# Heads 20 to 23 by rows through SyncE, moved memsets and another order of the opening steps of an attention-and-MLP kernel

## The chip, the cores and the metric

The kernel runs on one core of a Trainium2 chip. The metric is the device time of one execution in microseconds (us). The engines are TensorE (PE; PEld is its weight load), VectorE (DVE), ScalarE (ACT), GpSimd (POOL) and SyncE (SP). Each executes its own instructions in order. PE, DVE, ACT and POOL compute. SP issues DMAs and waits for semaphores, and POOL and ACT issue some DMAs as well.

## The reference

```python
def _attn_ref(q, k, v, s):                       # q, k, v: (8, 8, 576, 64); s: (8, 8, 576)
    scores = (1 / np.sqrt(D)) * np.matmul(q, k.transpose(0, 1, 3, 2))
    causal = np.triu(np.ones((S, S), dtype=bool), k=1)
    cum = np.cumsum(np.maximum(s, 0.0), axis=-1)
    bias = -(cum[:, :, :, None] - cum[:, :, None, :])
    scores = np.where(causal, -1e9, scores + np.minimum(bias, 0.0))
    attn = np.exp(scores - np.max(scores, axis=-1, keepdims=True))
    attn = attn / (np.sum(attn, axis=-1, keepdims=True) + 1e-09)
    return np.matmul(attn, v)

def _moe_ref(x, g_ln, w_ch1, w_ch2):             # x: (8, 576, 512), the heads side by side
    xn = (x - mean(x)) / np.sqrt(var(x) + 1e-06) * g_ln
    return x + np.maximum(xn @ w_ch1, 0.0) @ w_ch2     # w_ch1: 512 x 2048, w_ch2: 2048 x 512
```

So there are 8 batches of 8 heads, 64 heads in all, numbered through: head n belongs to batch n // 8. Causal attention with a bias from a cumulative sum is followed, per batch, by a layer norm, a two-layer MLP and a residual.

## The kernel before

**Attention.** Scores are computed transposed: keys on the partitions, queries along the free axis. A head has four full blocks of 128 keys and a last one of 64. The bias is not added: k and q each get four more rows (KA = 68 rows instead of 64) that hold the pieces of the cumulative sum in bf16 (high, middle, low part) and constants, so that the product of the 68 rows is score plus bias. `scores(b, h)` makes three PSUM banks `sa`, `sb`, `sc` and ACT takes the exponential into `er`; `scores_d` does the 64 x 64 corner for two heads. For heads up to 9 the causal mask is added by PE; from head 10 on POOL's `affine_select` (L345, L375) sets the masked part to zero after the exponential. `pv` multiplies with v, into which a column of ones gives the sum of the row, and `pv_norm` divides on DVE.

**Where k and q come from.** A group `gam` is four heads; three buffers `kq` hold k and q of a group, with the head dimension on the partitions. There are three ways into them:

- Batch 0 (groups 0 and 1) comes by tiles of 128 positions, eight heads wide, into `rowb`. PE transposes them (step T), DVE or ACT copies them out (step e).
- Groups 2 to `NPE` - 1 come by pairs of heads. POOL issues a casting DMA for k and one for q (`ld_cast_pair`), PE transposes each in six pieces (`tr_kind`, step Q), two copies on DVE or ACT take the result to `kq` (`evac_half`, step E), and four small DMAs on SP (`aug`) bring the bias rows.
- Groups from `NPE` on come by rows. SP issues ten loads of f32 rows into `rowtmp` (`ld_rows`, L169, k and q of five position tiles), POOL casts them and adds the bias columns (`cast_rows`, L177 and L180), and SP issues three DMA transposes into `kq` (`tr_rows`, L187). The keys and queries then stand in another layout, so `q_cols` splits a matmul that crosses position 512 in two.

`NPE` is 6 before the change, so groups 2 to 5 (heads 8 to 23) come by pairs.

**Layer norm and MLP.** `ln_xn` makes the normalized rows xn of a batch. One DMA transpose on SP (`ln_tr_dma`, L515) makes xT of a batch (from batch 1 on; batch 0 uses PE, step X). `mlp1` makes one of 16 blocks of the hidden layer (four matmuls of 512 columns, L538), `mlp2` a quarter of the second layer's sum for a tile of 128 positions (four matmuls, L557), and after the fourth quarter DVE makes the output tile `yo` and SP stores it. Such units stand in `queue`, and `run_units` takes them from there to fill PE between the steps of attention.

**The order of the work** is written out by hand. Up to head 17 it is the string PLAN: a word names a step, its arguments and perhaps the engine (`:D` DVE, `:A` ACT). The steps that the text speaks of: `W` matmuls on zeros that keep PE busy, `T.t.g` transposes of position tile t for group g, `S`, `x`, `V`, `N` scores, exponential, product with v and division for batch 0, `M.c.t.j` the first pieces of the MLP of batch 0, `Q`/`E` as above, `s.n`, `d.n`, `v.n`, `n.n` scores, corner, product with v and division of head n, `p.n` the function `pre(n)` (loads, `aug`, `tr_rows`, `ld_rows` that are due at head n), `c.n` the function `post(n)` (`cast_rows` that are due), `u` and `U` one unit of the queue, `D` the DMA transpose of batch 1's xT. There are 23 words `u` or `U`; "unit 20" is the 20th, which ends the second layer's sum of the first position tile and so leads to the first output. A loop over heads 18 to 63 follows, in which `pre`, `scores`, units, `post` and `pv_next` follow each other; the first units of batch 1 run at head 20.

POOL's instructions before PLAN (L636 to L682) are a list of DMA issues (k, q, v, weights) with memsets between them. A memset of rows 64 to 127 of `kq[2]` fills what the bias rows of heads 8 to 11 leave free, so the step `aug` waits for it.

SP in the built program before the change sends: s and one tile of k, aug of groups 2, 3, 4 and 5, two outputs, six loads of rows for group 6, xT of batch 1, one output, and on with groups 6 and 7.

Of the kernel before, what the change touches and what calls it, by code (L numbers as in the profile page):

```python
# [9 lines left out]
F32 = mybir.dt.float32  # L10
# [5 lines left out]
P = 128  # L16
# [3 lines left out]
def kernel(  # L20
# [11 lines left out]
    nc = tc.nc  # L32
    B, H, S, D = q.shape
# [5 lines left out]
    NF = S // P  # L39
# [6 lines left out]
    EW = 1664  # L46
    G = 4
    NG = BH // G
    NPE = 6
    NM = 10  # L50
    KT = 96
    QT = 6
# [32 lines left out]
    kq = [const.tile([P, 2, G, SP], BF16, name=f"kq{i}") for i in range(3)]  # L85


    def home(gam):
        return 2 if gam == 2 else gam % 2
# [38 lines left out]
    def tile_src(kind, t):  # L128
        pn = P if t < NF else TL
        src = k if kind == "k" else q  # L130
        return src[0, :, t * P : t * P + pn, :].rearrange("h s d -> s h d")

    def tile_dst(kind, t):
        pn = P if t < NF else TL
        u = "kq".index(kind)
        return rowb[0:pn, t, u * H : (u + 1) * H, 0:D]
# [9 lines left out]
    def ld_cast_tile(kind, t):  # L146
        nc.gpsimd.dma_start(out=tile_dst(kind, t), in_=tile_src(kind, t))

    def ld_cast(kind, g):
        ready[kind, g] = pair_tile(kind)  # L150
        nc.gpsimd.dma_start(out=ready[kind, g][0:QP], in_=pair_src(kind, g))

    def ld_cast_pair(g):
        ld_cast("k", g)
        ld_cast("q", g)

    def ld_cast_v(b, t):
        pn = P if t < NF else TL
        nc.gpsimd.dma_start(  # L159
            out=v_bf[b % 2][:pn, t, :, 0:D],  # L160
            in_=v[b, :, t * P : t * P + pn, :].rearrange("h s d -> s h d"),
        )

    def ld_rows(gam, t):
        pn = P if t < NF else TL
        b, h0 = gam // 2, (gam % 2) * G
        tmp = stage.tile([P, 2, G, D], F32, name="rowtmp", tag="st")
        for u, src in enumerate((k, q)):
            nc.sync.dma_start(  # L169
                out=tmp[0:pn, u],  # L170
                in_=src[b, h0 : h0 + G, t * P : t * P + pn, :].rearrange("h s d -> s h d"),
            )
        loaded["rows", gam, t] = tmp
# [10 lines left out]
    def tr_rows(gam, t0, t1):  # L184
        pn = P if t0 < NF else TL
        o, n = t0 * 2 * G * P, (t1 - t0) * 2 * G
        nc.sync.dma_start_transpose(  # L187
            out=kq[home(gam)]
            .rearrange("p u h s -> p (u h s)")[:, o : o + n * pn]
            .rearrange("p (h s) -> p h s", s=pn),  # L190
            in_=row_sets[gam % 2][0:pn, o : o + n * P],
        )
# [4 lines left out]
    def ld_w1(c):  # L197
        sl = slice(c * 512, (c + 1) * 512)
        nc.gpsimd.dma_start(out=w1_bf[:, :, sl], in_=w1_r[:, :, sl])

    def ld_w2(i):
        nc.gpsimd.dma_start(
            out=w2_bf[:, 4 * i : 4 * i + 4, :], in_=w2_r[:, 4 * i : 4 * i + 4, :]
        )
# [3 lines left out]
    def aug(gam, eng, h0=0):  # L208
        r = slice(gam * G + h0, gam * G + G)
        i = home(gam)  # L210
        eng.dma_start(out=kq[i][D : D + 1, 1, h0:G, 0:S], in_=c_hi[r, :])
        for j in range(3):
            eng.dma_start(out=kq[i][D + 1 + j : D + 2 + j, 0, h0:G, 0:S], in_=c3[r, j, :])
# [80 lines left out]
    def k_cols(b, h, kb):  # L294
        i, hh = home(b * 2 + h // G), h % G
        if b * 2 + h // G < NPE:
            return kq[i][0:KA, 0, hh, kb * P : (kb + 1) * P]
# [4 lines left out]
    def q_cols(b, h, q0, q1):  # L302
        i, hh = home(b * 2 + h // G), h % G
        if b * 2 + h // G < NPE:
            return [(q0, q1, kq[i][0:KA, 1, hh, q0:q1])]
# [330 lines left out]
    for t in range(1, NF):  # L636
        ld_cast_tile("k", t)
        ld_cast_tile("q", t)
        ld_cast_v(0, t - 1)
        if t == 1:  # L640
            make_identity(nc, ident)
        if t == 2:
            nc.gpsimd.memset(maskT, 0.0)
            nc.gpsimd.affine_select(
                out=maskT,
                in_=maskT,
                compare_op=ALU.is_ge,
                fill=-1.0e30,
                base=0,
                pattern=[[1, P]],  # L650
                channel_multiplier=-1,
            )
            nc.gpsimd.dma_start(out=gb, in_=moe_g_ln.partition_broadcast(P))
    ld_cast_v(0, NF - 1)
    ld_w1(0)
    ld_cast_pair(4)
    nc.gpsimd.memset(er[:, :, OD:EW], 0.0)
    nc.gpsimd.memset(v_bf[1][:, 0:NF, :, D : D + 1], 1.0)
    nc.gpsimd.memset(v_bf[1][0:TL, NF, :, D : D + 1], 1.0)
    for i in range(2):  # L660
        nc.gpsimd.memset(v_bf[i][TL:P, NF, :, :], 0.0)
    ld_cast_tile("k", NF)
    ld_cast_tile("q", NF)
    ld_cast_v(0, NF)
    ld_w1(1)
    for u, two in ((0, -1.0058441162109375), (1, 1.0019378662109375)):
        nc.gpsimd.memset(kq[2][D:P, u].bitcast(F32)[:, :, 0 : S // 2], two)
    for i in range(2):
        nc.gpsimd.memset(kq[i][0:KA, 0, :, S:SP], 0.0)
    ld_cast_pair(5)  # L670
# [18 lines left out]
    E = {"A": "act", "D": "dve"}  # L689
# [159 lines left out]

    AUGS = {8: 3, 9: 4, 16: 5}
    PAIR_LOADS = {12: (10, 9), 13: (11,)}


    def pre(n):
        if n == 11:
            ld_w2(2)
            ld_w2(3)
        for g in PAIR_LOADS.get(n, ()):  # L860
            ld_cast_pair(g)
        if n in AUGS:
            aug(AUGS[n], nc.sync)
        for gam in range(NPE, NG):
            if n - 4 * gam == -4:
                for t0, t1 in ((0, 2), (2, NF), (NF, NT)):
                    tr_rows(gam, t0, t1)
        for gam in range(NPE, NG):
            for t in ({-7: (0, 1, 2) if gam == NPE else (0, 1)} if gam % 2 == 0 else {-8: (0, 1), -7: (2, 3), -6: (4,)}).get(n - 4 * gam, ()):
                ld_rows(gam, t)  # L870
        for nb in range(2, B):
            t = n - H * nb + (4 if nb == 2 else 6)
            if 0 <= t < NT:
                ld_cast_v(nb, t)

    def post(n):
        for gam in range(NPE, NG):
            for t in {-6: (0, 1), -5: (2, 3, 4)}.get(n - 4 * gam, ()):
                cast_rows(gam, t)

    def pv_next():
# [56 lines left out]
        "U": lambda: run_units(1, True),  # L938
        "u": lambda: run_units(1),
        "p": lambda n: pre(n),  # L940
        "c": lambda n: post(n),
    }

    PLAN = """
        relu.0 scan.0 relur cq hi.0 scan.1 sub.0 hi.1 ck mid.0 lo.0 W.4 sub.1 mid.1 tc.0 bc.0 W.2
        T.0.0 scan.2 lo.1 hi.2 e.0.0:D T.0.1 W.2 e.0.1:D sub.2 tc.1 S.0.0.0 x.0.0.0 S.0.1.0
        bc.1 V.0.0 T.1.1 mid.2 N.0.0 x.0.1.0 T.1.0 V.0.1 e.1.1:D S.1.1.0 lo.2 m e.1.0:A tc.2 bc.2
        x.1.1.0 S.1.0.0 T.2.0 S.1.1.1 bc.4 T.2.1 e.2.0:D x.1.0.0 S.1.0.1 x.1.1.1 S.2.0.0 T.3.0
        V.1.1 N.0.1 e.2.1:D aug x.2.0.0 x.1.0.1 L.0 S.2.1.0 S.2.0.1 x.2.1.0 S.2.1.1 V.1.0
        e.3.0:D x.2.0.1 T.3.1 N.1.0 N.1.1 S.2.1.2 x.2.1.1 S.2.0.2 x.2.1.2 x.2.0.2 L.1 S.3.0.0  # L950
        X.0 V.2.1 S.3.0.2 N.2.1 y.0:A x.3.0.2 x.3.0.0 S.3.0.1 x.3.0.1 M.0.0.0 e.3.1:D V.2.0
        S.3.0.3 M.0.0.2 S.3.1.3 x.3.0.3 M.0.0.3 N.2.0 M.0.0.1 S.3.1.0 L.2 x.3.1.0 X.1 S.3.1.1
        y.1:D V.3.0 x.3.1.3 X.2 r.0.0:D M.0.1.0 M.0.1.1 T.4.0 N.3.0 S.3.1.2 M.0.1.3 y.2:A
        x.3.1.1 M.0.1.2 Q.k.4 e.4.0:D x.3.1.2 E.k.4.1:D S.4.0.1 r.0.1:A Q.q.4 x.4.0.1 T.4.1
        E.q.4.1:A E.k.4.0:D M.0.2.0 E.q.4.0:A S.4.0.0 M.0.2.2 M.0.2.3 e.4.1:D V.3.1 x.4.0.0
        N.3.1 M.0.2.1 S.4.1.1 L.3 x.4.1.1 s.8 Q.q.5 E.q.5.1:A S.4.1.0 Sk X.3 x.4.1.0 r.0.2:D
        E.q.5.0:A B.1.1 xk u Q.k.5 p.8 y.3:D u s.9 E.k.5.1:D d.8 E.k.5.0:D B.0.1 V.4.0 B.1.0 u u
        p.9 V.4.1 Z N.4.0 s.10 v.8 B.3.0 u u B.0.0 n.8 A.1 Q.q.6 N.4.1 v.9 Q.k.6 E.k.6.0:D
        E.q.6.0:A B.2.0 p.10 E.q.6.1:A E.k.6.1:D p.11 s.11 U n.9 A.0 u d.12 B.2.1 d.10 s.12 U u
        Q.k.7 Q.q.7 p.12 v.10 E.q.7.0:A E.q.7.1:A s.13 B.3.1 u E.k.7.0:D n.10 A.2 A.3 v.11 R  # L960
        E.k.7.1:D u s.14 d.14 n.11 p.13 U v.12 p.14 U O n.12 Q.k.8 g.0 Q.q.8 E.k.8.0:D E.q.8.1:A
        s.15 E.q.8.0:A U E.k.8.1:D u U v.13 Q.k.10 n.13 d.16 E.k.10.0:D p.15 s.16 u E.k.10.1:A
        v.14 n.14 p.16 s.17 Q.k.9 g.1 Q.q.10 U E.k.9.0:D E.q.10.0:A u E.q.10.1:A E.k.9.1:A v.15
        n.15 u g.2 Q.q.9 E.q.9.1:A U Q.k.11 u l.0 p.17 E.q.9.0:A Q.q.11 E.k.11.1:A E.k.11.0:D
        l.2 E.q.11.0:A E.q.11.1:A l.1 l.3 D
    """
    for word in PLAN.split():
        step, _, eng = word.partition(":")
# [6 lines left out]
    for n in range(2 * H + 2, BH):  # L975
# [11 lines left out]
        if h % 2 == 0:  # L987
            scores_d(b, h // 2)
        post(n)
        run_units(0 if late else 1)  # L990
        pv_next()
# [59 lines left out]
```

## Time and profile before

| | |
|---|---|
| time of the runs shown | 352.76 us median of 3 (352.19 to 354.0) |
| the profiled execution | 354.82 us, of which the span from the first to the last instruction is 353.1 |
| PE busy | 344.2 us (97%) in 3066 matmuls |
| DVE, ACT, POOL busy | 192.3, 188.3, 164.9 us |
| chain that ended last | PE 90%, DVE 4%, issue 2%, DMA 1% |
| DMA | 50.96 MB in 171783 packets, mean 144 GB/s |
| SP's queue, POOL's queue | 37.20 MB, 56.4% and 12.46 MB, 42.1% of 16 DMA engines' time |

The page gives the busy time of each engine, the span in 40 slices, the chain of instructions that ended last and groups of instructions by source line. The chain's "issue" is time in which an engine waited for nothing that the profile shows. Matmuls are pipelined and their ends are modelled, so a matmul of 512 columns shows as 379 ns while the next one starts 0.22 us after it.

### The profile page before, as it was taken

The page shows a single profiled execution, that of the slowest core. Times are in us where ns is not written, and L with a number is a line of the kernel's source. Part 1 is how long each engine was busy: PE and PEld are TensorE (multiplying, and loading weights), DVE is VectorE, ACT ScalarE, POOL GpSimd, SP SyncE. Part 2 cuts the span into 40 slices and gives each one's busy share as a digit, 9 for nine tenths or more (in the row PEclk, how much of TensorE's full clock was granted, in tenths as well). Part 3 has the DMA queues.
Part 4 walks back from the last instruction along what each step waited for, and adds up shares of the span by engine and source line. Part 5 has one row for each costly group of instructions (what it writes and reads, how often), then busy time and mean ns, then how long its engine had stood idle before and what let it go on. Part 6 is the DMA issues. An engine that isn't in the chain of part 4 may idle for free.

```text
span 353.1 us, 8167 instructions
## 1 busy us (share of the span) xinstructions
PE 344.2 (97%) x3066; PEld 196.5 (56%) x3090; DVE 192.3 (54%) x517; ACT 188.3 (53%) x360; POOL 164.9 (47%) x336
## 2 busy tenths in 40 slices
PE   8998999999999999999999999999999999999995
PEld 3897856555555455555555555555555544444444
DVE  7884788974366536653565549443844492113112
ACT  4797897957634674366616653576346502502500
POOL 8997578267465628465647275365621010000000
PEclk9998999999999999999999999999999999999999
DMA  9999999999999999999999999999740024011013
GB/s 140 170 176 140 199 203 125 144 186 182 183 180 164 215 164 180 215 223 181 182 177 213 162 192 203 195 173 198 144 125 2 3 65 128 2 59 59 2 31 89
DMA packets 171783, 50.96 MB, mean 144 GB/s; under 512 B 159520, under 2 KB 167136, under 8 KB 171744
## 3 DMA queue, kind: packets, MB, share of 16 engines
q1 hardware_dynamic: 117792, 37.20, 56.4%
q0 software_dynamic: 52432, 12.46, 42.1%
q10 hardware_dynamic: 1520, 0.79, 0.9%
q8 instruction: 24, 0.39, 0.5%
q14 instruction: 15, 0.12, 0.1%
HBM read 37.11 MB, written 9.44 MB: 132 GB/s over the span
## 4 chain that ended last, share of the span: by engine, by line
PE 90%; DVE 4%; issue 2%; DMA 1%; SPq 1%; POOL 1%; ACT 0%; POOLq 0%; DVEq 0%
PE py L557 32%; PE ph L538 31%; PE pot L403 7%; PE sc L325 3%; PE sa L325 3%; PE sb L325 3%; PE ph L820 2%; PE idle L612 2%; PE st L718 2%; DMA rowtmp<-in_q_dram 1%; PE trqk L275 1%; PE pot L776 1%; PE trt L696 1%; DVE xb L417 1%; DVE yo L568 1%
## 5 line engine op out<-in xcount | busy, mean ns | idle before, releaser
L557 PE MATMUL py<-w_bf,hT 128*128 128x512 bf16 (+2 forms) x584 | 130.9, 367 | 1.3
L538 PE MATMUL ph<-xT,w_bf 128*128 128x512 bf16 x480 | 112.6, 379 | 0.3 <-DVE hT L546 0.3
L548 ACT ACTIVATE hT<-ph 128x512 bf16<-128x512 f32 x102 | 60.8, 598 | 73.9 <-PE ph L538 73.9
L557 PEld LDWEIGHTS <-hT 128*128 128x128 bf16 x608 | 54.3, 98 | 52.6
L538 PEld LDWEIGHTS <-w_bf 128*128 128x128 bf16 x544 | 49.5, 98 | 51.6 <-issue 1.0
L336 ACT ACTIVATE er<-sa 128x512 bf16<-128x512 f32 x56 | 33.4, 596 | 63.4 <-PE sa L325 47.1
L345 POOL TENSOR_SCALAR_AFFINE_SELECT er<-er 128x256 bf16<-128x256 bf16 x108 | 45.4, 442 | 29.7 <-ACT er L336 28.9
L546 DVE TENSOR_SCALAR hT<-ph 128x512 bf16<-128x512 f32 x34 | 23.5, 691 | 57.9 <-PE ph L538 49.9
L568 DVE SCALAR_TENSOR_TENSOR yo<-py,rstd,xb 128x512 f32<-128x512 f32 x32 | 23.9, 748 | 35.2 <-PE py L557 33.9
L325 PEld LDWEIGHTS <-kq 68*128 68x128 bf16 x400 | 28.6, 97 | 21.7 <-issue 1.6
L403 PEld LDWEIGHTS <-er 128*128 128x128 bf16 x840 | 32.8, 98 | 13.0 <-POOL er L345 1.2
L403 PE MATMUL pot<-v_bf,er 128*128 128x65 bf16 x840 | 35.1, 194 | 0.4 <-POOL er L345 0.4
L159 POOL DMA_DIRECT2D v_bf<-in_v_dram x40 | 34.3, 864 | 2.0 <-PE pot L403 1.4
L336 ACT ACTIVATE er<-sc 128x512 bf16<-128x512 f32 x56 | 34.2, 611 | 0.0
L336 ACT ACTIVATE er<-sb 128x512 bf16<-128x512 f32 x56 | 33.5, 598 | 0.0
L177 POOL CAST kq<-rowtmp 128x512 bf16<-128x512 f32 (+1 forms) x25 | 15.7, 628 | 36.2 <-DMA rowtmp<-in_q_dram 36.1
L177 POOL CAST rowb<-rowtmp 128x512 bf16<-128x512 f32 (+1 forms) x25 | 15.3, 610 | 34.8 <-DMA rowtmp<-in_q_dram 19.5
L415 DVE RECIPROCAL rinv<-pot 128x5 f32<-128x5 f32 x56 | 10.8, 192 | 37.0 <-PE pot L403 37.0
L417 DVE TENSOR_TENSOR xb<-pot,rinv 128x256 f32<-128x256 f32 x56 | 23.8, 425 | 1.9
L493 DVE SCALAR_TENSOR_TENSOR xn<-xb,mv,gb 128x512 bf16<-128x512 f32 x28 | 22.9, 819 | 1.0
L325 PE MATMUL sa<-kq 68*128 68x512 bf16 x56 | 21.3, 381 | 1.5 <-issue 1.5
L447 DVE BATCH_NORM_STATS2 stats<-xb 128x6 f32<-128x128 f32 (+1 forms) x84 | 21.9, 321 | 0.3
(115 smaller groups left out, 354.4 us busy)
## 6 DMA issues: line engine op xcount, KB each, us to landing
out_dram<-yo SPq DMA_DIRECT2D x32, 256.0 KB
rowtmp<-in_k_dram SPq DMA_DIRECT2D x40, 128.0 KB
rowtmp<-in_q_dram SPq DMA_DIRECT2D x40, 128.0 KB
v_bf<-in_v_dram POOLq DMA_DIRECT2D x32, 128.0 KB, 5.7
w_bf<-in_moe_w_ch_dram POOLq DMA_DIRECT2D x8, 512.0 KB, 11.0
kp<-in_k_dram POOLq DMA_DIRECT2D x8, 144.0 KB, 7.9
qp<-in_q_dram POOLq DMA_DIRECT2D x8, 144.0 KB, 8.1
rowtmp<-in_k_dram SPq DMA_DIRECT2D x10, 64.0 KB
```

What stands on the lines that cost most here:

```text
L159: nc.gpsimd.dma_start(out=v_bf[b % 2][:pn, t, :, 0:D], in_=v[b, :, t * P : t * P + pn, :].rearrange("h s d -> s h d"),)
L177: nc.gpsimd.tensor_copy(out=rows[gam % 2][0:pn, t, :, :, 0:D], in_=loaded.pop(("rows", gam, t))[0:pn])
L325: nc.tensor.matmul(a[:, c + a0 - q0 : c + a1 - q0], lhsT=k_cols(b, h, kb), rhs=cols, start=True, stop=not (pe_mask and diag),)
L336: nc.scalar.activation(out=e[:, o : o + 512], in_=a, func=ACT.Exp, scale=scale)
L345: nc.gpsimd.affine_select(out=two, in_=two, compare_op=ALU.is_ge, fill=0.0, base=0, pattern=[[0, 2], [1, P]], channel_multiplier=-1,)
L403: nc.tensor.matmul(pot[:, t, :], lhsT=e[:, o : o + P], rhs=vv[:, kb, h, :], start=(kb == 0), stop=(kb == last),)
L417: nc.vector.tensor_tensor(out=xb[b][:, :, hs], in0=pot[:, 0:NF, 0:D], in1=rinv[:, 0:NF].unsqueeze(2).to_broadcast([P, NF, D]), op=ALU.mult,)
L538: nc.tensor.matmul(ph, lhsT=w1_bf[:, kd, fb * P : (fb + 1) * P], rhs=xT[:, :, kd, :], start=(kd == 0), stop=(kd == KD - 1),)
L546: nc.vector.tensor_scalar_max(out=hT[:, fb, :], in0=ph, scalar1=0.0)
L548: nc.scalar.activation(out=hT[:, fb, :], in_=ph, func=ACT.Relu)
L557: nc.tensor.matmul(py[t], lhsT=hT[:, fb, t * P : (t + 1) * P], rhs=w2_bf[:, fb, c0:c1], start=(fb == 0), stop=(fb == FB - 1),)
L568: nc.vector.scalar_tensor_tensor(out=yo, in0=py[t], scalar=rs, in1=x[:, c0:c1], op0=ALU.mult, op1=ALU.add)
```

## The change

- `NPE` becomes 5, so group 5 (heads 20 to 23) comes by rows: ten loads and three DMA transposes on SP and ten copies on POOL, in place of two pairs (four casting DMAs on POOL, 24 transposes on PE, eight copies on DVE and ACT) and aug of group 5. The loads are due at heads 14 and 15, the casts at 15 and 16, the transposes at 17. `q_cols` splits the matmuls of these heads.
- POOL's list before PLAN: `ld_w1(0)` comes ahead of the v tile 3; the memset of `kq[2]` comes right after pair 4, ahead of the last tiles of k, q and v; the memsets of `er` and `v_bf` come behind them.
- PLAN has another order. Up to step s.8 it holds the same PE steps; two copies of step e go from DVE to ACT (e.0.1, e.4.0) and two of step y from ACT to DVE. Q and E of pairs 10 and 11 are gone, c.15 and c.16 are new.
- In the loop, the two units that run ahead of the scores of every fourth head now run at head 24 too.

SP in the built program after the change sends: s and one tile of k, aug of groups 2, 3 and 4, ten loads of rows for group 5, one output, three transposes for group 5, six loads for group 6, one output, xT of batch 1, one output, and on. Each DMA of SP also waits for the one eight places before it.

```diff
-    NPE = 6
+    NPE = 5
...
+    ld_w1(0)
     ld_cast_v(0, NF - 1)
-    ld_w1(0)
     ld_cast_pair(4)
+    for u, two in ((0, -1.0058441162109375), (1, 1.0019378662109375)):
+        nc.gpsimd.memset(kq[2][D:P, u].bitcast(F32)[:, :, 0 : S // 2], two)
+    ld_cast_tile("k", NF)
+    ld_cast_tile("q", NF)
+    ld_cast_v(0, NF)
+    ld_w1(1)
     nc.gpsimd.memset(er[:, :, OD:EW], 0.0)
     nc.gpsimd.memset(v_bf[1][:, 0:NF, :, D : D + 1], 1.0)
     nc.gpsimd.memset(v_bf[1][0:TL, NF, :, D : D + 1], 1.0)
     for i in range(2):
         nc.gpsimd.memset(v_bf[i][TL:P, NF, :, :], 0.0)
-    ld_cast_tile("k", NF)
-    ld_cast_tile("q", NF)
-    ld_cast_v(0, NF)
-    ld_w1(1)
-    for u, two in ((0, -1.0058441162109375), (1, 1.0019378662109375)):
-        nc.gpsimd.memset(kq[2][D:P, u].bitcast(F32)[:, :, 0 : S // 2], two)
...
-    AUGS = {8: 3, 9: 4, 16: 5}
-    PAIR_LOADS = {12: (10, 9), 13: (11,)}
+    AUGS = {8: 3, 9: 4}
+    LD_FIRST = {-6: (0, 1), -5: (2, 3, 4)}
+    CAST_FIRST = {-5: (0, 1), -4: (2, 3, 4)}
+    PAIR_LOADS = {12: (9,)}
...
-            if n - 4 * gam == -4:
+            if n - 4 * gam == (-3 if gam == NPE else -4):
                 for t0, t1 in ((0, 2), (2, NF), (NF, NT)):
                     tr_rows(gam, t0, t1)
         for gam in range(NPE, NG):
-            for t in ({-7: (0, 1, 2) if gam == NPE else (0, 1)} if gam % 2 == 0 else {-8: (0, 1), -7: (2, 3), -6: (4,)}).get(n - 4 * gam, ()):
+            for t in ({-7: (0, 1, 2) if gam == NPE + 1 else (0, 1)} if gam % 2 == 0 else LD_FIRST if gam == NPE else {-8: (0, 1), -7: (2, 3), -6: (4,)}).get(n - 4 * gam, ()):
                 ld_rows(gam, t)
...
-            for t in {-6: (0, 1), -5: (2, 3, 4)}.get(n - 4 * gam, ()):
+            for t in (CAST_FIRST if gam == NPE else {-6: (0, 1), -5: (2, 3, 4)}).get(n - 4 * gam, ()):
                 cast_rows(gam, t)
...
     PLAN = """
...
-        S.3.0.3 M.0.0.2 S.3.1.3 x.3.0.3 M.0.0.3 N.2.0 M.0.0.1 S.3.1.0 L.2 x.3.1.0 X.1 S.3.1.1
-        y.1:D V.3.0 x.3.1.3 X.2 r.0.0:D M.0.1.0 M.0.1.1 T.4.0 N.3.0 S.3.1.2 M.0.1.3 y.2:A
...
-        Q.k.7 Q.q.7 p.12 v.10 E.q.7.0:A E.q.7.1:A s.13 B.3.1 u E.k.7.0:D n.10 A.2 A.3 v.11 R
-        E.k.7.1:D u s.14 d.14 n.11 p.13 U v.12 p.14 U O n.12 Q.k.8 g.0 Q.q.8 E.k.8.0:D E.q.8.1:A
-        s.15 E.q.8.0:A U E.k.8.1:D u U v.13 Q.k.10 n.13 d.16 E.k.10.0:D p.15 s.16 u E.k.10.1:A
-        v.14 n.14 p.16 s.17 Q.k.9 g.1 Q.q.10 U E.k.9.0:D E.q.10.0:A u E.q.10.1:A E.k.9.1:A v.15
-        n.15 u g.2 Q.q.9 E.q.9.1:A U Q.k.11 u l.0 p.17 E.q.9.0:A Q.q.11 E.k.11.1:A E.k.11.0:D
-        l.2 E.q.11.0:A E.q.11.1:A l.1 l.3 D
...
+        S.3.0.0 M.0.0.3 M.0.0.2 x.3.0.0 N.2.0 M.0.0.1 S.3.1.3 x.3.0.3 X.1 r.0.0:D x.3.1.3
+        S.3.1.1 S.3.1.0 T.4.0 V.3.0 y.1:D M.0.1.0 M.0.1.3 L.2 M.0.1.2 x.3.1.1 x.3.1.0 S.3.1.2
+        N.3.0 X.2 y.2:D M.0.1.1 Q.k.4 e.4.0:A x.3.1.2 S.4.0.1 Q.q.4 r.0.1:A M.0.2.0 x.4.0.1
...
+        B.2.1 n.8 Q.k.6 E.q.6.1:A E.k.6.1:D s.11 E.k.6.0:D U v.9 U d.12 d.10 n.9 s.12 u u Q.k.7
+        p.12 s.13 B.2.0 E.k.7.0:D B.0.1 v.10 Q.q.7 n.10 E.k.7.1:D A.0 p.13 E.q.7.1:A E.q.7.0:A U
+        A.2 u v.11 A.3 R s.14 p.14 c.15 n.11 u u v.12 U d.14 s.15 Q.q.8 u n.12 v.13 E.q.8.1:A
+        g.0 U Q.k.8 U p.15 n.13 E.k.8.1:D c.16 v.14 E.k.8.0:D g.1 E.q.8.0:A O U s.16 n.14 d.16
+        Q.k.9 u E.k.9.1:A p.16 v.15 Q.q.9 n.15 p.17 E.k.9.0:D E.q.9.0:A g.2 l.3 u E.q.9.1:A l.0
+        s.17 U l.1 l.2 U D
     """
```

## The prediction

> **What bounds the kernel now.** I read four views in turn: the page's busy shares, the engines' busy time over stretches of one clock period, TensorE's (PE's) timeline at its gaps, and the timelines of GpSimd (POOL) and SyncE (SP) around the instructions that release those gaps.
>
> ```profile
> PE 344.2 (97%) x3066; PEld 196.5 (56%) x3090; DVE 192.3 (54%) x517; ACT 188.3 (53%) x360; POOL 164.9 (47%) x336
> ...
> PEclk9998999999999999999999999999999999999999
> ...
> 26.70:30.11 3.41, 1.93 (x40) 1.59 (x37) 2.54 (x8) 2.03 (x5) 3.41 (x6) 1.00 1.36 144
> 30.11:33.52 3.41, 3.41 (x50) 3.41 (x47) 0.42 (x1) 3.36 (x7) 2.56 (x4) 0.50 2.61 142
> ```
>
> PE is the bound: it executes in order, and the time is its work plus its gaps. The last two lines (busy us of PE, PEld, DVE, ACT, POOL, then clock, DMA share, GB/s) show the one bad spot: PE works 1.93 of 3.41 us, and the next 3.41 us run at clock 0.50, so 1.7 us of work are lost there.
>
> ```profile
> 27.20 0.40 PE L718 MATMUL st<-kq 68*128 68x64 bf16 x8
> 29.07 0.38 PE L325 MATMUL sa<-kq 68*128 68x512 bf16 x1 [1.48 <-issue]
> ...
> 18.82 2.12 POOL L667 MEMSET kq<- 64x1152 f32 x2
> ...
> 20.96 0.76 SPq L211 DMA_DIRECT2D kq<-c  x1
> 21.78 1.82 SPq L213 DMA_DIRECT2D kq<-c  x3
> ```
>
> The gap stands before step s.8 (head 8). It is the bias rows of heads 8 to 11 (step aug): SP sends them at 20.96, as POOL's memset of the same rows ends at 20.94, and their last packet leaves at 28.3.
>
> Later the loads matter. Pair 7's k and q (issued at 34.20 and 35.95) took 11.3 and 10.3 us to land, so 45.5 and 46.3, and PE transposes them at 47.56: 2.1 us of slack. The last spot:
>
> ```profile
> 64.76 2.00 SPq L586 DMA_DIRECT2D out_dram<-yo  x2
> ...
> 70.06 0.51 SPq L169 DMA_DIRECT2D rowtmp<-in_q_dram  x1
> 71.79 1.88 SPq L515 DMA_TRANSPOSE xT<-xn  x1
> ...
> 75.71 0.62 PE L403 MATMUL pot<-v_bf,er 128*128 128x65 bf16 x15
> 76.23 1.02 PE L538 MATMUL ph<-xT,w_bf 128*128 128x512 bf16 x4
> ```
>
> SP issues two outputs, six loads of head rows, then the transpose of batch 1's xT. The first matmul that reads this xT starts at 76.23, 4.4 us after the issue; in the trace's semaphore events the last part of xT lands at 76.19. So PE meets it with no slack.
>
> **Part by part: the sum.** It is made on the profiled execution: span 353.1, 354.82 with what lies outside.
>
> *PE work.* Four tr_kind steps go: 24 transposes, 12 of which take 0.51 us on the chain, so -1.0 us. Heads 20 to 23 now read k and q in the split form: head 28's eight matmuls take 0.66 us (111.63 to 112.29) where head 20's five take 0.65, so +0.04 for four heads. Eight copies of 0.80 leave ACT and DVE (six and two); both are half idle, so nothing. The four issues of aug 5 (0.6 each) leave SP. POOL gains 4.1 us of casts (five of 0.61 and five of 0.21) and loses four issues of 0.63; its busy share in 50 to 70 leaves room, and the casts stand behind the masks of s.14 and s.15 and ahead of those of s.16, which PE reads only after 65. Nothing, if the rows have landed by then.
>
> *The memsets.* The memset of the bias rows starts where the memset of er did, 14.27, and ends at 16.4; the rows, with the same 7.4 us from there to the last packet, arrive at 24. PE's work from 6.5 to s.8 is the same set of steps, so s.8 could come at 27.4. But the new order puts T.4.0 before V.3.0, M.0.1.x and X.2: 1.15 us of PE work earlier, 22.05 instead of 23.20. It reads row tile 4, whose q part was issued at 16.73 and took 6.3 us: 23.03. With its issue 0.35 later (2.12 us of memset instead of 1.77) that is 23.0 to 23.4. PE waits there 1.0 to 1.4 us, and s.8 follows 5.15 us of work later, at 28.5: 0.6 earlier than before. The first weights ahead of a v tile, the swapped evacuations (two to ACT, two to DVE, 0.4 to 1.0 us each) lie under PE's work, and cost up to 0.5 if they don't.
>
> *The clock.* With that gap halved and moved to an earlier stretch I take the half-speed stretch as gone: -1.7 us by pair 7.
>
> *Pair 7.* Q.k.7 keeps its place: 16.7 us of work after s.8, so 45.2. That is before the data of 45.5, and the data come later too. SP now sends ten loads of rows as soon as aug 4 is out, from about 36, while POOL's queue is full (204 GB/s in 36 to 46). There a packet of POOL's queue takes 90 ns (2227 packets, 124.6% of 16 engines, 10 us), one of SP's 18 ns (2404 packets, 110.5%, 69.5 to 72). In 87 to 93, where both queues are loaded, they moved 2381 and 3063 packets, so about turn by turn. Equal turns make POOL's queue 20% slower: 9.5 us become 11.4, and pair 7 lands at 47.4. Bounds: 45.5 with no delay, 48.3 at 30%. I take 47.5 for Q.k.7, level with 47.56 before: what the opening gained goes into this wait.
>
> The Trainium skill ("DMA: Bandwidth & Descriptors", queues, rings and completion order) says that each DMA engine takes turns between its queue rows by whole packets of several descriptors. By that rule the delay could be several times mine if SP's turns hold more descriptors; the 87 to 93 row speaks for nearly equal ones.
>
> *xT.* From Q.k.7 to the end of unit 20, which feeds the first output, there are 15.0 us of work: 62.5 (before: 63.70). From there SP in the new program does: output, three transposes for heads 20 to 23, six loads, output, xT. Rows: 1.06 us until the output is issued (63.70 to 64.76) and 0.4 for it; three transposes 6.7 (the set of 95.59; others 6.3 to 9.2, and 5.6 from the median and shortest rows); six loads 3.8 (66.81 to 70.57); one output 0.4; xT until the first reader 4.4. That is 16.7 us, between 15.3 and 18.3. PE has 12.7 us of work in the same stretch (12.53 before). So the first reader waits 4.0 us and starts at 62.5 + 16.7 = 79.2 instead of 76.23: +3.0. PE's queue stands behind it whole. The work that follows is the same.
>
> A gap of 4.0 us is longer than the one at 27.6, so the half clock comes back after it. Part of the slow stretch lies in the gap itself: 0 to 1.7 us, I take 1.2.
>
> Sum: +3.0 + 1.2 = +4.2 us of 353.1, from -0.3 (Q.k.7 at 45.6, chain 15.3, no slow clock) to +7.2 (48.3, 18.3, 1.7). The profiled execution stands 2.06 above the median of the timed runs (352.19 to 354.0); I carry the difference over: 352.76 + 4.2 = 357.0.
>
> The Trainium skill ("TensorE: Matmul & The Clock Gate", why this matters for your kernels) asks for no gaps over about 3 us in PE's work, or the clock drops. By that rule the 1.48 us gap would have been free and only the xT wait is charged; the trace gated after 1.93 busy of 3.41, so here the measurement decides, and the shorter waits at T.4.0 and Q.k.7 may be charged too (second rival).
>
> **The rivals.**
> *Faster: the new SP order has room.* If the three transposes take 5.6 us or less, the loads go out behind them without waiting, and pair 7 lands at 45.5, PE never waits for xT: 60.6 + 12.7 = 73.3 for the first reader, -2.9, and 349.9. It decides at a chain under 12.7 us, and no set of three transposes in this trace is short enough with the rest. For it: loads at 36 find SP idle for 20 us, so the casts are early. Chance 0.12.
> *Slower still: the waits add up.* Rows are served in longer turns, so pair 7 lands 2 us later than I say, the transposes take 7.9 as at 78.12 while v tiles share the engines, or the waits at T.4.0 and Q.k.7 gate the clock: +2.5 to +4 on the forecast, 360. Chance 0.17.
> *No change that can be told: the xT wait is small.* Q.k.7 at 45.6 and a chain of 15.3 give a first reader at 75.9, and a slow clock of 0 to 1.7: 352.5 to 354. For it: DVE is freed of copies, so outputs may be ready sooner. Chance 0.21.
> *The forecast,* a late xT between 75.9 and 81 with its clock: 354.5 to 359. Chance 0.50.
>
> **How the numbers follow.** 0.5% (1.8 us) is about what a measurement of this kernel can tell from no change. Slower by more: 0.50 + 0.17 + 0.02 of the small wait = 0.69; within: 0.19; faster: 0.12. The range leaves out most of the faster case and the top of the slower one: 351.0 to 361.0; the likeliest case alone has 354.5 to 359.
>
> **What would show it.** Right: no gap before s.8 over 0.5 us and clock 1.00 in 30 to 33.5; a gap before T.4.0 near 22 and one before Q.k.7 near 45; SP's xT transpose issued 12 us or more after unit 20's end, and a gap of 2 to 6 us before the first L538 matmul of batch 1, with a slice of PEclk under 9 behind it. Wrong: xT issued before 72, no gap there, and PE's busy sum down by 1 us with nothing in its place.

## The result, and the profile after

The kernel after takes 363.06 us (median of 5 runs, 362.47 to 364.7), the kernel before 352.40 us (5 runs, 351.32 to 354.0). The ratio is 1.031, with a 95% interval of 1.027 to 1.035: slower by 3.1%, some 10.7 us. The profiled execution of after took 363.06 us, with a span of 361.3.

From the page: the busy times of the engines, the granted clock in 40 slices, the shares of the chain that ended last.

```profile
PE 345.3 (96%) x3078; PEld 195.0 (54%) x3078; DVE 193.5 (54%) x517; ACT 182.8 (51%) x352; POOL 164.7 (46%) x342
...
PEclk9999999996999999999999999999999999999999
...
PE 76%; DMA 11%; POOL 5%; SPq 3%; DVE 2%; issue 2%; POOLq 0%
```

PE is not busier in any way that matters (345.3 us against 344.2, and its clock is halved for longer). The chain changed: DMA has 11% of it instead of 1%, SP's queue 3% instead of 1%. One slice of the clock is at 6, the one from 81 to 90 us. The opening, which had the slow stretch before, is clean.

PE's timeline at the place where batch 1's MLP begins:

```profile
70.42 0.19 PE L403 MATMUL pot<-v_bf,er 128*128 128x65 bf16 x1 [1.76 <-DMA v_bf<-in_v_dram]
...
75.74 0.62 PE L403 MATMUL pot<-v_bf,er 128*128 128x65 bf16 x15
82.34 6.14 PE L538 MATMUL ph<-xT,w_bf 128*128 128x512 bf16 x16 [5.98 <-DMA xT<-xn]
88.32 0.38 PE L325 MATMUL sa<-kq 68*128 68x512 bf16 x1
```

Up to 75.74 PE runs level with the kernel before (s.20 starts at 75.03, before at 75.00). Then it stands for 5.98 us, until xT has landed; before, its first reader started at 76.23. The clock of the same stretch (us, busy PE, PEld, DVE, ACT, POOL, clock, DMA share, GB/s):

```profile
76.50:80.66 4.16, 0.00 (x0) 0.00 (x0) 1.48 (x5) 0.72 (x3) 3.32 (x9) 1.00 1.31 229
80.66:84.08 3.42, 1.74 (x5) 0.64 (x5) 0.00 (x0) 0.00 (x0) 0.00 (x0) 0.50 1.40 258
84.08:87.49 3.41, 3.41 (x10) 1.21 (x9) 0.69 (x1) 0.60 (x1) 2.90 (x6) 0.50 1.16 190
```

The clock is halved from 80.66 to 87.49, and PE is busy for 5.15 us of it. So the sixteen matmuls behind the wait take 5.98 us until s.21.

SP's timeline shows what xT stood behind:

```profile
44.49 3.24 SPq L169 DMA_DIRECT2D rowtmp<-in_q_dram  x1
...
62.66 0.37 SPq L586 DMA_DIRECT2D out_dram<-yo  x1
63.22 8.72 SPq L187 DMA_TRANSPOSE kq<-rowb  x3
72.00 0.58 SPq L169 DMA_DIRECT2D rowtmp<-in_k_dram  x1
...
75.42 0.44 SPq L586 DMA_DIRECT2D out_dram<-yo  x1
75.97 3.47 SPq L515 DMA_TRANSPOSE xT<-xn  x1
```

The first output is issued at 62.66 and the transposes of heads 20 to 23 take SP 8.72 us. Then come the six loads and an output, and only at 75.97 xT, though its rows xn were ready near 71.1. It is read 6.4 us later. The first line is one of the ten row loads: where a load took SP about 0.5 us before, these took up to 3.24 each, and the last of the ten landed at 64.67.

### The profile page after: what moved, and what is told of

Its sections match the earlier page's. It is cut to its first block, busy times and chain, and to the rows that moved or that the text cites. A ratio compares the mean times of both kernels' runs of the same rounds, so it can differ in the third digit from the quotient of the medians.

```text
span 361.3 us, 8183 instructions
## 1 busy us (share of the span) xinstructions
PE 345.3 (96%) x3078; PEld 195.0 (54%) x3078; DVE 193.5 (54%) x517; ACT 182.8 (51%) x352; POOL 164.7 (46%) x342
## 4 chain that ended last, share of the span: by engine, by line
PE 76%; DMA 11%; POOL 5%; SPq 3%; DVE 2%; issue 2%; POOLq 0%
PE ph L538 31%; PE py L557 29%; PE pot L403 5%; SPq L169 3%; DMA rowtmp<-in_q_dram 3%; DMA xT<-xn 3%; PE sc L325 3%; PE sa L325 3%; PE sb L325 3%; DMA rowb<-in_q_dram 2%; DMA kq<-c 2%; POOL rowb L147 2%; DMA v_bf<-in_v_dram 1%; POOL v_bf L159 1%; POOL kq L658 1%
## 5 line engine op out<-in xcount | busy, mean ns | idle before, releaser
L557 PE MATMUL py<-w_bf,hT 128*128 128x512 bf16 (+2 forms) x608 | 134.0, 368 | 0.0
L538 PE MATMUL ph<-xT,w_bf 128*128 128x512 bf16 x480 | 114.8, 385 | 6.8 <-DMA xT<-xn 6.8
L345 POOL TENSOR_SCALAR_AFFINE_SELECT er<-er 128x256 bf16<-128x256 bf16 x108 | 44.5, 431 | 32.4 <-ACT er L336 31.6
L325 PEld LDWEIGHTS <-kq 68*128 68x128 bf16 x412 | 29.4, 97 | 20.8 <-issue 0.5
L177 POOL CAST rowb<-rowtmp 128x512 bf16<-128x512 f32 (+1 forms) x30 | 18.3, 611 | 35.7 <-DMA rowtmp<-in_q_dram 31.3
L415 DVE RECIPROCAL rinv<-pot 128x5 f32<-128x5 f32 x56 | 10.7, 191 | 33.8 <-PE pot L403 33.8
L493 DVE SCALAR_TENSOR_TENSOR xn<-xb,mv,gb 128x512 bf16<-128x512 f32 x28 | 24.7, 882 | 1.0
L325 PE MATMUL sc<-kq 68*128 68x256 bf16 (+1 forms) x200 | 21.7, 226 | 0.0
```

What stands on the lines that cost most here:

```text
L177: nc.gpsimd.tensor_copy(out=rows[gam % 2][0:pn, t, :, :, 0:D], in_=loaded.pop(("rows", gam, t))[0:pn])
L325: nc.tensor.matmul(a[:, c + a0 - q0 : c + a1 - q0], lhsT=k_cols(b, h, kb), rhs=cols, start=True, stop=not (pe_mask and diag),)
L345: nc.gpsimd.affine_select(out=two, in_=two, compare_op=ALU.is_ge, fill=0.0, base=0, pattern=[[0, 2], [1, P]], channel_multiplier=-1,)
L493: nc.vector.scalar_tensor_tensor(out=xn, in0=tiles[t], scalar=mvs[b][:, t, 0:1] if b > 0 else mean0[:, t : t + 1], in1=gb, op0=ALU.subtrac ...
L538: nc.tensor.matmul(ph, lhsT=w1_bf[:, kd, fb * P : (fb + 1) * P], rhs=xT[:, :, kd, :], start=(kd == 0), stop=(kd == KD - 1),)
L557: nc.tensor.matmul(py[t], lhsT=hT[:, fb, t * P : (t + 1) * P], rhs=w2_bf[:, fb, c0:c1], start=(fb == 0), stop=(fb == FB - 1),)
```

## The experiments

All times below are medians; each ratio is to the kernel before, run beside it on the same chip (its medians were 352.4 to 353.6). "Transposes" is the time from the first to the end of the last of group 5's three on SP; the last two columns are the issue of xT and the start of its first reader on PE, all from the profiled executions.

| kernel | us | ratio (95%) | transposes | xT issued | first reader |
|---|---|---|---|---|---|
| before | 352.4 | | none | 71.79 | 76.23 |
| after | 363.06 | 1.031 (1.027 to 1.035) | 8.7 | 75.97 | 82.34 |
| e1 memsets | 352.37 | 0.999 (0.997 to 1.001) | none | 69.62 | 74.07 |
| e2 rows | 361.97 | 1.024 (1.020 to 1.028) | 8.6 | 76.42 | 80.97 |
| e3 order, pairs | 359.61 | 1.017 (1.012 to 1.023) | none | 71.84 | 81.88 |
| e4 xT ahead of loads | 358.05 | 1.014 (1.010 to 1.017) | 8.6 | 72.12 | 77.02 |
| e5 busy while waiting | 362.21 | 1.027 (1.022 to 1.033) | 8.8 | 75.47 | 83.18 |
| e6 new opening | 354.12 | 1.003 (1.000 to 1.006) | none | 72.01 | 76.44 |
| e7 rows cast by DMA | 364.57 | 1.033 (1.031 to 1.036) | 8.9 | 76.22 | 83.03 |
| e8 loads early | 362.79 | 1.029 (1.025 to 1.033) | 9.0 | 78.14 | 83.86 |
| e9 e4, old opening | 357.52 | 1.016 (1.012 to 1.019) | 9.3 | 72.97 | 77.42 |
| e10 half the rows | 361.74 | 1.027 (1.023 to 1.031) | 7.4 | 74.40 | 80.95 |
| e11 transposes alone | 361.81 | 1.027 (1.022 to 1.031) | 7.4 | 76.39 | 80.95 |
| e12 loads alone | 357.56 | 1.014 (1.010 to 1.019) | none | 73.34 | 77.89 |
| e13 v tile later | 362.08 | 1.024 (1.019 to 1.029) | 7.8 | 77.62 | 82.98 |
| e14 half, v later | 360.30 | 1.019 (1.015 to 1.023) | 7.4 | 75.67 | 80.88 |
| e15 after again | 363.82 | 1.031 (1.027 to 1.034) | 8.6 | 75.87 | 82.89 |

Theory A, behind most of the expectations: the transposes and loads that stand ahead of xT in SP's queue cause the loss. Its rivals were the order of the plan (C) and the fill of the DMA engines (D).

**e1: the memsets alone, in the kernel before.**

```
+    ld_w1(0)
     ld_cast_v(0, NF - 1)
-    ld_w1(0)
     ld_cast_pair(4)
+    for u, two in ((0, -1.0058441162109375), (1, 1.0019378662109375)):
+        nc.gpsimd.memset(kq[2][D:P, u].bitcast(F32)[:, :, 0 : S // 2], two)
...
```

> The kernel before with one part of the change: the list of POOL instructions ahead of the plan (memset of the bias rows early, first weights ahead of a v tile). Theory A (the opening is a plain gain and the loss comes from the rows alone): the gap of 1.48 us before s.8 falls under 0.4 us, the granted clock is 1.00 in 30 to 33.5, T.4.0 waits up to 0.8 us, and the time falls by 1.5 to 3 us, to 349.5 to 351. Rival B (given back later): s.8 comes 1 us or more earlier, but Q.k.7 then waits for pair 7, which still lands near 45.5 to 46.5, and the time is within 1 us of 352.4.

The gap before s.8 went, s.8 came at 28.17 (before 29.07), the clock was 1.00 in 30 to 33.5, and every later step came 2 to 3 us earlier than in the profile of before: the span is 350.1. Yet the median moved by 0.7 us, which can't be told from nothing. Of the 13 runs of before beside it, all had a mean clock of 0.997 or more, where the profiled execution had 0.995. That execution was slower than all 13 of them (351.33 to 354.13). The slow stretch that the change removes there hardly occurs in the timed runs. Theory A has the profile and not the time; rival B has the time and not its reason, for Q.k.7 does not wait.

**e2: the rows alone, in the kernel before.**

```
-    NPE = 6
+    NPE = 5
...
-        ... Q.k.10 ... E.k.10.0:D ... Q.k.11 ...
+        ... c.15 ... c.16 ...
```

> The kernel before with only heads 20 to 23 taken by rows (loads due at heads 14 and 15, casts at 15 and 16, transposes at 17); POOL's list and the order of the plan stay. Theory A (xT of batch 1 stands on SP behind the three transposes and six loads): the first matmul that reads it starts at 81 to 83.5 instead of 76.2, the clock halves after it, and the time is 360 to 364, so all of the loss is here. Rival C (the new order of the plan is what costs): the first reader comes at 77 to 79 and the time is 353 to 356.

Theory A holds in the time: 8.9 us of the 10.7, with the old order and the old POOL list. The place is only partly as expected. The first reader came at 80.97, but 3.75 us were already lost at 71.40, where v.16 waited for a v tile that POOL had issued behind the casts of late rows:

```profile
71.40 0.19 PE L403 MATMUL pot<-v_bf,er 128*128 128x65 bf16 x1 [3.75 <-DMA v_bf<-in_v_dram]
```

**e3: the new order with pairs.** Heads 20 to 23 go back to pairs in the new plan, with the steps Q and E of pairs 10 and 11 put in by hand.

> The kernel after with heads 20 to 23 put back to pairs (24 transposes on PE, eight copies, bias rows by four DMAs on SP); POOL's list and the new order of the plan stay. Theory A: SP has no rows to load before 60 and sends xT at 71 to 73; its first reader starts within 0.5 us of 75 to 77 and the clock stays at 1.00 behind it; 349.5 to 353. Rival C (the order costs): the waits at T.4.0 and at the pairs add up, and the time is 355 or more.

It took 359.61 us (ratio 1.017), which reads as the rival. But in its profile PE waits 1.11 and 1.69 us at those inserted transposes, for work on ACT, and the clock halves behind them. So it measures where I put the steps and not the order of the change. e6 takes its place for the steps up to s.8.

**e6: the new order up to s.8 only,** with the plan of before from there on, on e1.

> The kernel of the first experiment (the kernel before with the changed list of POOL) with the new order of the plan up to step s.8, and the old order from there on; heads 20 to 23 come by pairs. Theory A (the new order of the opening costs only its wait at T.4.0): s.8 comes 0.5 to 1.3 us later than in the first experiment (28.17), and the time is 352.5 to 354. Rival C (the new order of the opening costs much): 355 or more.

354.12 us, ratio 1.003 (1.000 to 1.006) against 0.999 (0.997 to 1.001) for e1, so about 1.4 us, at the edge of what these runs can tell. PE's timeline shows what it is:

```profile
24.20 0.36 PE L696 MATMUL trt<-ident,rowb 96*68 96x96 bf16 x4 [1.87 <-DMA rowb<-in_k_dram]
25.17 0.36 PE L696 MATMUL trt<-ident,rowb 96*68 96x96 bf16 x4 [0.61 <-DMA rowb<-in_q_dram]
```

T.4.0 stands too early for the tile that it reads. So the opening is not the bulk of the loss; what it costs fits this wait. No run tests the order behind s.8 and the two units at head 24 by themselves. e2, which has the old order, leaves 1.8 us of the 10.7 for them, the opening and POOL's list together.

**e4: xT ahead of group 6's loads,** in the kernel after: the six loads due at p.17 are issued behind D.

```
-        s.17 U l.1 l.2 U D
+        s.17 U l.1 l.2 U D G          (G issues the loads; pre(17) no longer does)
```

> The kernel after with one thing changed: the six loads of rows for heads 24 to 27 go out on SP behind the transpose of batch 1's xT instead of ahead of it. Theory A (order on SP): xT is issued at 72 to 72.5 instead of 75.97, its first reader starts at 78 to 79 instead of 82.34, the slow clock shrinks from 2.6 to some 1.2 to 2 us, and the time is 357 to 359.5. Rival D (the DMA engines are full, so xT lands when the backlog is through): the first reader comes within 1.5 us of 82.3 and the time is 361.5 or more.

```profile
62.84 8.54 SPq L187 DMA_TRANSPOSE kq<-rowb  x3
...
72.12 3.07 SPq L515 DMA_TRANSPOSE xT<-xn  x1
```

xT goes 3.9 us earlier, its reader 5.3 us earlier than in after, the clock stays at 1.00, and 5 us of the 10.7 come back by moving six loads behind one DMA. So theory A holds for this half. What remains in its profile are waits at v.16 (1.5 us, for a v tile), at xT (1.2), at head 20's product with v (1.4, for a mask on POOL behind casts of group 6, whose loads are now later) and at the next part of xT (0.9).

**e11: the three transposes alone,** added to e1, where nothing needs them.

```
     def pre(n):
+        if n == 17:
+            tr_extra()        # tr_rows of group 5's sizes, from rowb into kq[2]
```

> The kernel of the first experiment (old order, changed list of POOL, heads 20 to 23 by pairs, 0.999 of the time before) with three DMA transposes more on SP, of the same size as group 5's, put where the change has them: between the outputs and group 6's six loads. Their result is not used; no load, cast or step of PE is added. Theory A (these transposes on SP ahead of xT are the cost): they take 6.3 to 8.8 us, xT is issued at 75.5 to 78.5 instead of 69.6, its first reader starts at 80 to 83 instead of 74.1, and the time is 358 to 363. Theory D (the row loads and casts are the cost): the transposes take less than 6 us with nothing else in flight, and the time is 352 to 356.

SP's timeline, then PE's:

```profile
64.67 7.38 SPq L860 DMA_TRANSPOSE kq<-rowb  x3
...
76.39 2.43 SPq L515 DMA_TRANSPOSE xT<-xn  x1
```

```profile
80.95 5.48 PE L538 MATMUL ph<-xT,w_bf 128*128 128x512 bf16 x16 [6.89 <-DMA xT<-xn]
86.27 0.38 PE L325 MATMUL sa<-kq 68*128 68x512 bf16 x1
```

Three instructions on SP that no computing engine executes cost 2.7%. xT is issued 6.8 us later than in e1 and read 6.9 us later (74.07 to 80.95), and the clock halves. That is the main mechanism by itself, without loads, casts or another order.

**e12: the ten row loads alone,** added to e1; nobody reads them.

> The kernel of the first experiment with ten loads of rows more on SP, where the change has them (due at heads 14 and 15). Nobody reads them; no cast, transpose or step of PE is added, and the pairs of heads 20 to 23 are still loaded, so this is the loads on top of everything. Theory D (the loads' bytes delay what POOL loads behind them): pairs 9 to 11 land at 60 to 66 instead of 56 to 59.5, PE waits for them, and the time is 355 to 360. Theory A (only SP's order ahead of xT costs): the loads are out of SP by 57, xT is issued within 1 us of 69.6, and the time is 352 to 354.

357.56 us, a ratio of 1.014, so theory D has a part too:

```profile
58.93 0.43 PE L275 MATMUL trqk<-ident,kp 96*128 96x96 bf16 x6 [1.95 <-DMA kp<-in_k_dram]
```

The pairs land late, and SP, held up in the loads, sends the bias rows, outputs and loads behind them late, so xT goes at 73.34. These loads are on top of the pairs, where the change puts them in the pairs' place, so this may overstate what they cost there.

**e10: half the rows,** in the kernel after.

```
-        for u, src in enumerate((k, q)):
+        for u, src in enumerate((k,) if gam == NPE else (k, q)):
```

> The kernel after with only the five loads of k for heads 20 to 23; their q rows are made from the k rows, so half of the loaded bytes and five of SP's issues are left out, and the scores of these heads are other numbers. Everything else stays. Theory D (the loads' bytes fill the DMA engines, so casts, v tile and the transposes come late): the last cast ends by 62, the v tile of head 16 is hardly waited for, the three transposes take 7.5 us or less, the first reader of xT comes at 79 to 81, and the time is 358.5 to 361.5. Theory A (SP's order alone; a set of three transposes takes as long in any case): the casts come earlier, but the transposes still take 8.3 to 9 us from their start near 63, the first reader stays at 81.5 to 83, and the time is 362 to 363.5.

361.74 us, with an interval that overlaps that of after. The transposes took 7.4 us instead of 8.7, v.16 no longer waited, and the first reader came at 80.95 instead of 82.34. Between the theories: the bytes of the loads may be worth up to 1.3 us in the transposes. This rests on one profile each, and e13 below, with all the rows, has 7.8.

**e7: the rows by casting DMAs** on POOL, in the kernel after: `nc.gpsimd.dma_start` from k and q straight into the bf16 rows, without `rowtmp` and without the casts.

> The kernel after with the rows of heads 20 to 23 loaded by ten casting DMAs of POOL straight into the bf16 rows, in place of ten f32 loads on SP and five casts on POOL; the copies of the bias columns, the transposes and all orders stay. It writes half the bytes and no instruction of POOL waits for the loads. Theory G (the f32 row loads fill the DMA engines, so casts, v tile and transposes come late): the rows land by 62, the v tile of head 16 is not waited for, the three transposes end at 69 to 70 instead of 72, xT is issued at 72.5 to 74.5, its first reader starts at 77.5 to 79.5, and the time is 356.5 to 360. Theory A without G (SP's order alone): the transposes still end at 71 or later and the time is 361 to 363.

The forecast of theory G fails: no cast waits for a load any more, and the transposes still take 8.9 us and the first reader comes at 83.03. But its condition was not met either. POOL issues these loads at 53.02 to 61.76, where SP had them at 38.24 to 56.81, and the last lands at 66.2 by the trace's semaphore events, after the 64.67 of the kernel after and not by 62. So this run does not decide on theory G. POOL's ten issues of 0.67 to 0.81 us stand ahead of the v tiles, v.16 waits 2.57 us, and the clock halves there as well.

**e8: group 6's loads early,** ahead of the first output, in the kernel after; one v tile moved ahead of casts.

> The kernel after with group 6's six loads on SP ahead of the first output and of group 5's transposes (they were between these and xT), and the v tile that stood behind the last casts of group 5 on POOL ahead of them. Theory A: xT is issued near 71.5 to 72.5 and its first reader starts at 76.5 to 77.5, as in the experiment with these loads behind xT; the waits for the v tile of head 16 (1.5 us) and for the mask at 89 (1.4 us), which that one had, go, and the time is 354.5 to 357. Rival D (more loads in the full DMA engines make the rows of group 5 later still): the transposes end after 72.5 and the time is 358 or more.

Rival D holds: SP is still in the loads at 67, the first output goes at 67.15 instead of 62.66, and the transposes end at 77.4. The v tile that was issued 8.5 us earlier (58.38) landed at 70.95, no earlier than before its move (70.38). Here, with six more loads in the queues at the same time, issuing it earlier did not deliver it earlier.

**e9: e4 with the old opening.**

> The kernel of the fourth experiment (the kernel after with group 6's six loads behind xT, 1.0135 of the time before) with the old order of the plan up to step s.8. Theory A (the new opening's wait at T.4.0 costs 1.1 to 1.8 us, as the sixth experiment has it, and adds to the rest): 356 to 357. Rival (the gain of the opening is given back at the waits for xT and the v tile, which end when DMAs land): 357.5 to 358.5.

357.52 us, ratio 1.016 (1.012 to 1.019), against 1.014 for e4. The time is the rival's, and its reason is not shown. In this profile the old opening gained nothing that could be spent later: T.4.0 waits 0.72 and 0.63 us here too, and s.8 comes at 29.09, against 28.50 in e4.

**e5: PE kept busy while it waits,** in the kernel after.

```
+        if late: keep_warm(26)
         run_units(2 if late else 0, True)
```

> The kernel after with 26 matmuls on zeros (512 columns, some 0.22 us each, 5.7 us in all) put ahead of the first matmul that reads batch 1's xT, so that PE is busy while it waits. Nothing else is changed. Theory A (the wait itself costs 6.1 us and the slow clock behind it 2.6): the first reader still starts near 82.3, the granted clock is 1.00 throughout, and the time falls by 2 to 3 us, to 360 to 361. Rival E (the clock's part is small, since other engines set the pace while PE is slow): the clock is 1.00, but the time is 362 to 363.5. Rival F (the matmuls on zeros delay what follows): more than 363.5.

```profile
75.78 5.77 PE L612 MATMUL idle<-zeros 128*128 128x512 bf16 x26
83.18 3.69 PE L538 MATMUL ph<-xT,w_bf 128*128 128x512 bf16 x16 [1.63 <-DMA xT<-xn]
86.71 0.38 PE L325 MATMUL sa<-kq 68*128 68x512 bf16 x1
```

With PE busy the clock stays at 1.00, and from the first reader to s.21 it takes 3.53 us instead of 5.98: the half clock costs 2.45 us. In this execution xT came 0.84 us later than in after, so the span gained only 1.4. The medians differ by less than 1 us and their intervals overlap (1.022 to 1.033, 1.027 to 1.035), so the time alone does not settle it; the two profiles do, for this stretch.

**e13, e14, e15: what made xT itself slow.** In after, e5, e7 and e10 xT took 6.4 to 7.7 us from its issue to its reader, and POOL issued a v tile some 2 us behind it. e13 sends that tile 10 us later, e14 does the same with half the rows, e15 is the kernel after again.

```
-            if 0 <= t < NT: ld_cast_v(nb, t)
+            for tt in {(3, 1): (), (3, 2): (1, 2)}.get((nb, t), (t,)): ...
```

> The kernel after with one v tile of batch 3, which POOL issued at 77.70, 1.7 us behind the transpose of xT, issued together with the next v tile at head 20 (near 87). Theory V (that v tile shares the DMA engines with xT and holds it up): xT takes 4.4 to 5 us from its issue to its first reader instead of 6.4, the first reader starts at 80 to 81.2, and the time falls by 1 to 2 us against the kernel after. Rival W (the six loads that stand right ahead of xT on SP hold it up): it stays at 6 us or more, and the time is that of the kernel after within 0.8 us.

> The kernel of the experiment with half the rows (only k is loaded for heads 20 to 23, q is made from it) with the same v tile moved. Theory V with D: both terms that the prediction's chain had too small are gone; transposes 7 to 7.6 us, xT 4.4 to 5 us to its first reader, which starts at 78.5 to 79.8, where the prediction had it (79.2), and the time is 2.5 to 4 us under that of the kernel after. Rival W: first reader at 80.5 or later, and at most 2 us under the kernel after.

> The kernel after, unchanged, beside the two others on the same chip: 362 to 364.5 us, transposes 8.2 to 9 us, xT 6 to 7 us from its issue to its first reader at 81.5 to 83.5, clock 0.985 to 0.991. If xT takes 5 us or less here, the v tile is no cause and the term varies from run to run.

xT to its reader: 7.0 us in e15, 5.4 in e13, 5.2 in e14. So without this v tile it is 1.0 to 1.8 us shorter than in after and e15. But a v tile behind xT is not enough: in before, e1, e2, e6, e11 and e12 POOL issued one 1.9 to 2.7 us behind xT as well, and there xT took 4.4 to 4.6 us. What sets these six apart on SP is that no output goes out right ahead of xT. In after, e5, e7, e10 and e15 an output of 256 KB goes 0.5 to 0.6 us ahead of it and a v tile follows (6.4 to 7.7 us); with such an output and no v tile right behind (e4, e8, e9, e13, e14) it is 4.5 to 5.7. No run moves the output alone, so its part stays open.

The first readers came later than expected: 82.98 in e13 (80 to 81.2) and 80.88 in e14 (78.5 to 79.8). In e13's profile the clock halves from 25.51 to 28.93, behind waits of 1.06 and 0.50 us at T.4.0, and s.8 comes at 31.99. In time e13 is 0.7% under e15, with intervals that overlap, and e14 1.1%, with intervals that don't (ratios 1.024, 1.019 and 1.031).

## Why the prediction was right or wrong

It forecast slower by way of a late xT, and that is what happened, by the mechanism that it named: SP's order output, transposes, loads, output, xT, and a half clock behind the wait. The size was wrong: 357.0 (351 to 361) against 363.06. The steps, in its order:

- *Memsets, s.8 and the first half clock.* The gap before s.8 went (0.22 us left), the clock is 1.00 in 30 to 33.5, T.4.0 waits 0.74 and 0.85 (forecast 1.0 to 1.4). s.8 came at 29.51 instead of 28.5; other executions of the same opening had 28.50 to 29.26 (seven), and 30.39 to 31.99 (e6, e13, e14). Right in kind. But the 1.7 us were credited against an execution that was slower than the timed runs of before.
- *Pair 7.* Forecast at 47.4, landed at 46.80, and PE did not wait. It was already under way when SP's loads began at 38.24. The delay fell on what POOL issued behind it: three weight loads after 38 took a median of 11.5 us to land before, and 15.3 now. The rule of the Trainium skill that the prediction weighed there ("DMA: Bandwidth & Descriptors", queues, rings and completion order: turns by whole packets) allowed for pair 7 to come later still; the trace has it earlier than the forecast.
- *The casts: "Nothing, if the rows have landed by then."* They had not: the last three waited 3.22, 1.78 and 0.43 us, POOL's v tile behind them went at 66.85, and PE waited 1.76 for it. By the profile that wait costs nothing up to the first reader, in after and in e4, since PE then stands at xT anyway (5.98 and 1.23 us).
- *The chain from unit 20 to the first reader.* This is the step that failed. Unit 20 ended at 61.60 (forecast 62.5), and the chain took 20.7 us instead of 16.7 (range to 18.3). Two terms were too small. The three transposes took 8.7 us, where the sum has 6.7 from one set of before. Sets of the kind that the change adds (`kq<-rowb`) took 6.3 to 7.4 there, so the row was of the right kind and at the lower end for the place: e11 has 7.4 there without the rows, e10 7.4 with half of them, e13 7.8 with all. What makes the rest of the 8.7 stays open. The other term is xT to its reader: 4.4 was the row of before, and it was 6.4. 1.0 us of that went with the v tile in e13, in an order that also has an output right ahead of xT, unlike before. With half the rows and the v tile later, e14's chain is 80.88 - 62.61 = 18.3 us, the upper end of the range.
- *The half clock behind it.* Forecast 1.2, "0 to 1.7"; 2.45 by e5. The prediction allowed for one slow stretch of 3.41 us; two came in a row.
- *The sum.* First reader +6.11 instead of +3.0, clock +2.45 instead of +1.2, the rest -0.3: +8.24 on the profiled execution of before, against +4.2. (The upper bound of the sum, by its own terms, is 48.3 + 15.0 + 18.3 - 76.23 + 1.7 = +7.1 and not +7.2, which changes nothing.)
- *The base.* "I carry the difference over" took 2.06 us off. 354.82 + 8.24 is 363.06, the median itself. The kernel after profiled at its median; the kernel before profiled 2 us above its own, with a slow stretch that its runs mostly lack. Without that step the forecast would have been 359.0.

SP's timeline of before has these sets of three transposes, among others; the second is the 6.7 of the sum:

```profile
78.12 7.89 SPq L187 DMA_TRANSPOSE kq<-kq  x3
95.59 6.70 SPq L187 DMA_TRANSPOSE kq<-rowb  x3
...
188.93 9.24 SPq L187 DMA_TRANSPOSE kq<-kq  x3
```

The rival "slower still: the waits add up" (360, chance 0.17) was nearest. Of its mechanisms one happened in part: the transposes were longer, though no run shows that v tiles held them up. Pair 7 was not later, and in the profile of after no clock was halved behind T.4.0 or Q.k.7; in e13's it was, behind T.4.0.

No version with rows was faster than the kernel before. The shortest of all is e1, and its gain can't be told from none.

The DMA queues between 38 and 65 us show a part of why rows cost more than the PE work that they save. First before, then after; queue, packets, MB, share of 16 engines (POOL's is q0, SP's q1):

```profile
q0 software_dynamic: 8939, 4.23, 120.3%
...
q1 hardware_dynamic: 75, 0.04, 0.7%
```

```profile
q0 software_dynamic: 7258, 3.44, 97.4%
q1 hardware_dynamic: 4932, 1.42, 33.7%
```

Together 131.1% instead of 121.0% (packets overlap, so it can exceed 100%): the queues were well filled before, and there are 10 points more of packet time in these 27 us. What a cast, v tile or transpose waits for comes through these queues.

## What to carry to other kernels

When a change puts instructions into the queue of an engine that "only issues", list everything that already waits its turn there, and follow the one that the busy engine will read next; three DMA transposes ahead of a fourth cost 2.7% here with no other change, and moving six loads behind it gave half of the loss back. Price a DMA from all rows of its kind, and take the long ones where the DMA engines are already full. And before a profile's slow stretch is credited as a gain, compare that execution with the timed runs: if it is the slowest of them, the stretch may not be in the others.

## What the runs showed of the hardware that was not expected

- With POOL's queue full (97.4% of 16 engines' time from 38 to 65), a row load in after held SP's queue for up to 3.24 us, against some 0.5 at 72 to 75, and landed up to 16 us after its issue (issued at 44.49, its cast starts at 60.98).
- A wait of 2.57 us on PE was followed by a clock of 0.60 in the next 3.4 us (e7, 70.4 to 73.8); one of 1.95 us in e12 was not, and one of 1.48 in the profile of before was. The Trainium skill ("TensorE: Matmul & The Clock Gate", HAM oscillation) speaks of gaps over about 3.4 us; the first and the last do not agree with it, and the measurement decides.
- The same DMA transpose (xT) took 4.4 to 4.6 us until its reader with a v tile of 128 KB issued some 2 us behind it (six executions), and 6.4 to 7.7 us with an output of 256 KB right ahead of it as well (five). With the output and no such v tile it took 4.5 to 5.7 (five). The two were not varied one by one in one order.
